# Last expert's rows weighed and scattered straight to the output; attention product, loads, weighing and stores placed between expert steps

## The chip, the cores and the metric

The kernel runs on one core of one Trainium2 chip. The metric is the time of one execution on the device, in microseconds (us).

## The reference

A normalized input goes through two branches that are added to it: linear attention with a learned feature map, and a mixture of eight experts of which each token takes two. S = 2048 tokens, D = 512, 32 heads of 16, F = 1792.

```python
# x: (1, 2048, 512)
xn = layernorm(x)
# attention branch
q, k, v = split_heads(xn @ wqkv)
phi_q = concat(softmax(q @ w_phi), softmax(-(q @ w_phi)))      # the same for k
num = phi_q @ (phi_k^T v);  den = phi_q . sum(phi_k) + 1e-6
A = merge_heads(num / den) @ wo
# expert branch
gates = softmax(xn @ wg); take the top 2 of 8, divided by their sum -> cw
y_e = gelu(xn @ w1[e]) @ w2[e]
B = sum over the two experts of cw * y_e
return x + A + B
```

## The kernel before

All matrix products run in three passes over split operands (a high and a low part, `hi*hi + lo*hi + hi*lo`, `mm3`, lines L162 to L164), so a logical product of 512 columns is three matmuls.

**Stages.** The first part normalizes, computes queries, keys, values and gates, and sorts tokens into slots of experts. Experts are then taken in order of size, each with a fixed number of rows (its cap). One of four plans of caps is chosen at run time by a branch; each has its own copy ("arm") of the code below. In the runs here it is the first: 556, 544, 540, 528, 520, 512, 504, 492.

**Steps.** Each expert has 14 steps (`FB`), one for 128 of the 1792 hidden columns, so there are steps s = 0 to 111. A step issues, in this order: `load_we(s+5)` on SP (weights), `split_we(s+2)` (ACT cast L256, DVE subtraction L259, the high and low parts), `layer1(s)` (12 matmuls into a bank pH, gelu on ACT L1171, cast L1173, DVE subtraction L1176 giving the split h), then a list of other work put there with `at(step, function, ...)`, then `layer2(s-1)`. An expert whose cap is at most 512 uses `layer2_rows`: 12 matmuls of 512 columns (L1211) that add into four banks pY of 128 rows; in the expert's last step they are sorted by bank, so that a bank is complete every three matmuls. The banks are then copied out, in turn by ACT and DVE (`row_copy`, L1192), and each is scattered by POOL to the DRAM tensor `y_rows`, where each token has its two rows (`scatter`, L1184). For the last expert the four scatters follow at once; for others they are spread over later steps (`leave`).

**Work between the steps.** For each of 16 query blocks u the list holds `q_sub`, `q_exp`, `q_den` and `q_turn` (a DVE transpose, L1118) in steps that follow each other; `numer(c, g)` then takes two transposed blocks: eight matmuls into banks pN (L1135), four from each block. The last, `numer(3,1)`, stands in step 99 and needs the blocks 14 and 15. `load_wo`, `split_wo` bring and split the output weights, `load_r` brings the residual rows, `split_o` splits the attention's result for the output product.

**After the steps.** `attended(t)` for 16 tiles of 128 tokens: 12 matmuls into a bank pO. `load_y(t)` brings both rows of each token of the tile from `y_rows` in one DMA of 512 KB (L1290), which waits for the last scatters; `weigh(t)` scales one row by its gate on ACT (L1474), adds the other with its gate on DVE (L1475) and adds both to the residual (L1477); the bank pO is added (L1469, L1492), and SP stores the tile (L1494).

**Order.** SP, PE, ACT and DVE run in the order in which the code is written; POOL's order comes from the framework's scheduler. Tiles in SBUF come from a pool of slots ("keptN" and "keptR" are two kinds of them).

Of the kernel before, what the change touches and what calls it, by code (L numbers as in the profile page):

```python
# [35 lines left out]
def kernel(  # L36
# [34 lines left out]
    xsr = xs.rearrange("(r a) f -> r (a f)", a=4)  # L71
    xe = nc.dram_tensor("x_slots", (2, STRIDE, D), F32, kind="Internal").ap()
# [1086 lines left out]
    def layer1(s):  # L1159
# [14 lines left out]
        if gw > cap > 4 * P and b == 0:  # L1174
            nc.vector.memset(f32(h[:, cap:gw]), 0.0)
# [15 lines left out]
    def row_copy(i, y, ps):  # L1191
        (nc.vector.tensor_copy if i % 2 else nc.scalar.copy)(  # L1192
            y.rearrange("p (a i c) -> p a i c", a=4, c=32),
            ps.rearrange("p (i a c) -> p a i c", a=4, c=32))

    def layer2_rows(s):

        e, b = divmod(s, FB)
        cap, gw = CAPS[e], GW[e]
        n = -(-cap // P)  # L1200
        m = [min(P, cap - i * P) for i in range(n)]
# [14 lines left out]
        for i in range(n):  # L1216
            if i % 2 == 0:
                y = slot([P, 2, D], name="y")
            row_copy(i, y[0:m[i], i % 2], yb[e][i][0:m[i]])
            to = (y[0:m[i], i % 2], sidx[0:m[i], e * TPE + i:e * TPE + i + 1], ys)  # L1220
            if e == E - 1:
                scatter(*to)
            else:
                at(s + 2 + i, leave, *to)
            if i % 2:
                free(y) if e == E - 1 else at(s + 2 + i, free, y)
        free(*yb.pop(e))

    def layer2(s):
# [3 lines left out]
        if cap <= 4 * P:  # L1233
            return layer2_rows(s)
# [107 lines left out]
    at(94, load_wo)  # L1342
    at(98, split_wo, 0)
    at(99, split_wo, 1)
    for i, t in enumerate((106, 108, 110, 111)):
        at(t, split_o, *divmod(i, 2))

    for i in range(NQ // 2):
        at(max(73 + 3 * i, QS[2 * i + 1] + 6), numer, *divmod(i, 2))
    for t in range(0, NT, 2):  # L1350
        at(106 + t // 4, load_r, t)
# [62 lines left out]
    state = [wraw, wsp, gx, tx, xg, gr, step, kvp, ek, kr, vt, qt, km, qs, ot, oh, ol, ht, yb, scat, xr, yg,  # L1414
# [12 lines left out]
    def experts(caps):  # L1427
# [18 lines left out]


        AHEAD = 8
        EARLY = 4

        def attended(t):
            c, j = divmod(t, TPC)
            ps = bank("pO")
            mm3(ps, [(oh[c, b // 2][:, b % 2, j * P:(j + 1) * P], ol[c, b // 2][:, b % 2, j * P:(j + 1) * P],
                      woh[b // 2][:, b % 2, :], wol[b // 2][:, b % 2, :]) for b in range(KD)])
            if j == TPC - 1:
                for g in range(2):
                    free(oh.pop((c, g)), ol.pop((c, g)))
            return ps

        first = attended(0)
        for t in range(AHEAD):
            load_y(t)
        for g in range(2):
            split_o(2, g)
        for t in range(EARLY):
            o = xr[t // 2][:, t % 2, :]
            ps = attended(t) if t else first
            nc.vector.tensor_add(o, o, ps)  # L1469
            free(ps)  # L1470

        def weigh(t):
            y = yg.pop(t)
            nc.scalar.activation(y[:, 0, :], y[:, 0, :], AF.Copy, scale=cw[:, t, 0:1])  # L1474
            nc.vector.scalar_tensor_tensor(y[:, 0, :], y[:, 1, :], cw[:, t, 1:2], y[:, 0, :], op0=ALU.mult, op1=ALU.add)  # L1475
            o = xr[t // 2][:, t % 2, :].rearrange("p (i a c) -> p i a c", a=4, c=32)
            nc.vector.tensor_add(o, o, y[:, 0, :].rearrange("p (a i c) -> p i a c", a=4, c=32))  # L1477
            free(y)

        late = {}  # L1480
        for t in range(NT + 1):
# [62 lines left out]
```

## Time and profile before

| | |
|---|---|
| median of 3 runs | 881.64 us (881.12 to 882.27) |
| the profiled execution | 881.75 us |
| its span | 879.8 us |
| busy: PE, DVE, ACT, POOL | 870.0, 665.5, 439.0, 148.6 us |
| granted TensorE clock, mean | 0.997 of full speed |
| attention product, first to last matmul | 828.5 to 872.6 us |

The span is the time from the first to the last instruction of the profiled execution; the rest of its own time lies around it. "Busy" counts what an engine executed, and idle time of an engine that nobody waits for costs nothing. The chain that ended last is followed back from the last instruction to what released it at each step.

### The profile page before, as it was taken

The numbers are of one execution on the slowest core, as the hardware profiler recorded it, in microseconds if no ns is written. First come the engines' busy times: TensorE is split into PE (matmuls) and PEld (weight loads), VectorE is DVE, ScalarE is ACT, GpSimd is POOL, SyncE is SP. The second block draws the span as 40 slices with busy tenths as digits, with TensorE's granted clock in tenths as the row PEclk, the third lists the DMA queues.
The fourth block names the chain that finished last, engine by engine and source line by source line (L and its number), as shares of the span: only waits on it lengthen the run. The fifth ranks groups of instructions, "written<-read, shape, count | busy, mean of one in ns | idle before, by whom it ended". The sixth has DMA issues, their size and how long they took to land.

```text
span 879.8 us, 15861 instructions
## 1 busy us (share of the span) xinstructions
PE 870.0 (99%) x5879; PEld 769.8 (87%) x5879; DVE 665.5 (76%) x1089; ACT 439.0 (50%) x721; POOL 148.6 (17%) x201
## 2 busy tenths in 40 slices
PE   9999999999999999999999999999999999999996
PEld 7888878899999999999999999987777778788885
DVE  6889898878774568788779877878887888534477
ACT  4454412734734464556654665645565456544341
POOL 5000002100004113411331141114222200000200
PEclk9999999999999999999999999999999999999998
DMA  8320115674218331843463354425632744750196
GB/s 280 106 96 6 46 34 169 166 210 133 84 59 247 115 114 55 237 124 108 138 212 109 108 189 132 145 89 191 177 123 89 226 140 137 234 194 1 40 343 242
DMA packets 119479, 124.34 MB, mean 141 GB/s; under 512 B 9704, under 2 KB 84200, under 8 KB 119392
## 3 DMA queue, kind: packets, MB, share of 16 engines
q1 hardware_dynamic: 113168, 105.72, 37.6%
q0 software_dynamic: 6224, 17.51, 6.2%
q8 instruction: 48, 0.79, 0.4%
q14 instruction: 39, 0.32, 0.1%
HBM read 97.30 MB, written 25.89 MB: 140 GB/s over the span
## 4 chain that ended last, share of the span: by engine, by line
PE 91%; DVE 5%; issue 1%; DMA 1%; ACT 1%; POOL 0%; SPq 0%; ACTq 0%; DVEq 0%; POOLq 0%
PE pY L1211 13%; PE pH L162 12%; PE pH L163 12%; PE pH L164 12%; PE pY L1246 6%; PE pY L1252 6%; PE pY L1247 6%; PE pY L1249 2%; PE pY L1248 2%; PE pY L1254 2%; PE pV L162 2%; PE pV L164 2%; PE pV L163 2%; PE pQ L451 1%; PE pQ L449 1%; PE pQ L450 1%
## 5 line engine op out<-in xcount | busy, mean ns | idle before, releaser
L1171 ACT ACTIVATE gl<-pH 128x278 f32<-128x278 f32 (+7 forms) x182 | 78.5, 440 | 249.3 <-PE pH L164 239.8
L1176 DVE TENSOR_TENSOR h<-gl,h 128x556 fp32r<-128x556 f32 (+7 forms) x112 | 78.7, 703 | 123.6 <-ACT h L1173 98.4
L1211 PE MATMUL pY<-ws,h 128*128 128x512 f32 x340 | 87.9, 395 | 0.9 <-ACT gl L1171 0.9
L1211 PEld LDWEIGHTS pY<-ws,h 128*128 128x128 f32 x340 | 62.6, 186 | 21.3 <-ACT gl L1171 7.1
L163 PE MATMUL pH<-keptR,ws 128*128 128x270 f32 (+3 forms) x248 | 75.2, 303 | 0.0
L162 PE MATMUL pH<-keptR,ws 128*128 128x270 f32 (+3 forms) x248 | 75.2, 303 | 0.0
L164 PE MATMUL pH<-keptR,ws 128*128 128x270 f32 (+3 forms) x240 | 74.0, 308 | 0.0
L1173 ACT CAST h<-gl 128x556 fp32r<-128x556 f32 (+7 forms) x112 | 70.7, 631 | 3.6
L162 PE MATMUL pH<-xgh,ws 128*128 128x272 f32 (+3 forms) x220 | 70.9, 322 | 0.0
L163 PE MATMUL pH<-xgl,ws 128*128 128x272 f32 (+3 forms) x220 | 70.8, 322 | 0.0
L1184 POOL DMA_INDIRECT y_rows<-keptN,pidx x39 | 43.3, 1110 | 154.8 <-ACT gl L1171 143.3
L1246 PE MATMUL pY<-h,ws 128*128 128x416 f32 (+4 forms) x176 | 62.0, 352 | 0.0
L1184 POOL DMA_INDIRECT y_rows<-keptN,sidx x16 | 19.4, 1210 | 249.4 <-ACT gl L1171 92.2
L164 PE MATMUL pH<-xgh,ws 128*128 128x264 f32 (+3 forms) x188 | 59.7, 318 | 0.0
L1247 PE MATMUL pY<-h,ws 128*128 128x412 f32 (+4 forms) x160 | 55.6, 347 | 0.0
L256 ACT CAST keptR<-keptN 128x1024 fp32r<-128x1024 f32 (+3 forms) x68 | 45.9, 712 | 6.8 <-DVE keptN L952 6.8
L163 PEld LDWEIGHTS pH<-keptR,ws 128*128 128x128 f32 x248 | 46.7, 188 | 2.8
L162 PEld LDWEIGHTS pH<-keptR,ws 128*128 128x128 f32 x248 | 46.8, 189 | 1.8
L164 PE MATMUL pH<-xgh,keptR 128*128 128x272 f32 (+3 forms) x148 | 47.7, 322 | 0.0
L1184 POOL DMA_INDIRECT y_rows<-yq,pidx x27 | 29.4, 1089 | 105.7 <-ACT gl L1171 99.9
L164 PEld LDWEIGHTS pH<-keptR,ws 128*128 128x128 f32 x240 | 45.2, 188 | 1.9
L927 POOL DMA_INDIRECT keptN<-xn_rows,tidx x28 | 31.3, 1117 | 88.3 <-PE pV L164 49.3
(339 smaller groups left out, 2426.7 us busy)
## 6 DMA issues: line engine op xcount, KB each, us to landing
keptN<-in_B_w_dram SPq DMA_DIRECT2D x142, 256.0 KB
wr<-in_B_w_dram SPq DMA_DIRECT2D x82, 256.0 KB
keptN<-y_rows SPq DMA_DIRECT2D x16, 512.0 KB
x_slots<-keptN SPq DMA_DIRECT2D x24, 256.0 KB
keptN<-x_slots SPq DMA_DIRECT2D x40, 128.0 KB
keptN<-in_A_x_dram SPq DMA_DIRECT2D x16, 256.0 KB
xn_rows<-keptN SPq DMA_DIRECT2D x16, 256.0 KB
keptN<-in_A_x_dram SPq DMA_DIRECT2D x8, 512.0 KB
```

What stands on the lines that cost most here:

```text
L162: nc.tensor.matmul(ps, lh, rh, start=(i == 0), stop=False)
L163: nc.tensor.matmul(ps, lh, rl, start=False, stop=False)
L164: nc.tensor.matmul(ps, ll, rh, start=False, stop=(i == n - 1))
L256: nc.scalar.copy(dst_h, src)
L1171: step[:] = [nc.scalar.activation(g[:, c:c + m], ps[:, :m], AF.Gelu_apprx_tanh)]
L1173: nc.scalar.copy(h[:, 0:cap], g)
L1176: nc.vector.tensor_sub(h[:, gw:], g, f32(h[:, 0:cap]))
L1184: i = nc.gpsimd.indirect_dma_start(out=to, out_offset=bass.IndirectOffsetOnAxis(ap=rows, axis=0), in_=y, in_offset=None)
L1211: nc.tensor.matmul(yb[e][i][0:m[i]], h[:, o:o + m[i]], v[z], start=(b == 0 and low + z == 0), stop=(b == FB - 1 and low > 0))
L1246: nc.tensor.matmul(ps[i][:, 0:w - P], vh, h[:, P:w], start=st, stop=False, skip_group_check=True)
L1247: nc.tensor.matmul(ps[i][:, 0:m], vl, h[:, P:cap], start=False, stop=False, skip_group_check=True)
L1252: nc.tensor.matmul(ps[i][:, 0:m], v[0][:, i * P:(i + 1) * P], h[:, gw + P:], start=False, stop=sp_, skip_group_check=True)
```

## The change

The attention product, the loads from `y_rows`, the weighing and the stores no longer stand after the steps. They are spread over the last expert's steps: `attended` over 99 to 106, `load_y` over 99 to 105, `weigh` over 101 to 107, `store` over 102 to 108, with counts for each step. What prepares them stands earlier: `load_wo` (93, was 94), `split_wo` (96 and 97, were 98 and 99), `load_r` (96 to 103, were 106 to 109), `split_o` (98, 100, 102, 103), and `numer(3,1)` in step 97, where it was in 99.

The last expert's rows do not go through `y_rows`. Its rows of `y_rows` are set to zero by four scatters (`last_zero`), so the weighing adds nothing for them. Its gates are gathered by slot into `w7` by way of a small DRAM tensor `cw_rows`. In step 110 the output rows already stored are gathered by slot (`last_base`). When a bank pY of the last expert is complete, one DVE operation computes pY times gate plus base (`last_rows`, L1320 in the changed kernel), and one POOL scatter writes the rows to the output; slots without a token point beyond the output and are dropped by the bounds. The expert before the last now has the four immediate scatters. In the plan that runs, the caps 504 and 492 become 512.

```diff
 PLANS = (
-    (556, 544, 540, 528, 520, 512, 504, 492),
...
+    (556, 544, 540, 528, 520, 512, 512, 512),
...
@@ -1196,9 +1197,7 @@
     def layer2_rows(s):
 
         e, b = divmod(s, FB)
-        cap, gw = CAPS[e], GW[e]
-        n = -(-cap // P)
-        m = [min(P, cap - i * P) for i in range(n)]
+        n = 4
         if b == 0:
             yb[e] = [bank("pY") for _ in range(n)]
         h = ht.pop(s)
...
-            o = low * gw + i * P
-            nc.tensor.matmul(yb[e][i][0:m[i]], h[:, o:o + m[i]], v[z],
+            o = (low * n + i) * P
+            nc.tensor.matmul(yb[e][i], h[:, o:o + P], v[z],
...
         free(h, *ws)
         if b < FB - 1:
             return
         for i in range(n):
+            if e == E - 1:
+                last_rows(i, yb[e][i])
+                continue
             if i % 2 == 0:
                 y = slot([P, 2, D], name="y")
-            row_copy(i, y[0:m[i], i % 2], yb[e][i][0:m[i]])
-            to = (y[0:m[i], i % 2], sidx[0:m[i], e * TPE + i:e * TPE + i + 1], ys)
-            if e == E - 1:
+            row_copy(i, y[:, i % 2], yb[e][i])
+            to = (y[:, i % 2], sidx[:, e * TPE + i:e * TPE + i + 1], ys)
+            if e == E - 2:
                 scatter(*to)
             else:
                 at(s + 2 + i, leave, *to)
             if i % 2:
-                free(y) if e == E - 1 else at(s + 2 + i, free, y)
+                free(y) if e == E - 2 else at(s + 2 + i, free, y)
         free(*yb.pop(e))
 
     def layer2(s):
 
         e, b = divmod(s, FB)
         cap, gw = CAPS[e], GW[e]
-        if cap <= 4 * P:
+        if cap == 4 * P:
             return layer2_rows(s)
         if b == 0:
             yb[e] = [bank("pY") for _ in range(5)]
@@ -1277,6 +1279,55 @@
 
     def leave(y, rows, to):
...
+    LC = (E - 1) * TPE
+    rows7 = cp.tile([P, 3, 4], I32, name="rows7")
+    w7 = cp.tile([P, 4], F32, name="w7")
+
+    def last_index():
+
+        nc.vector.tensor_scalar(rows7[:, 0], sidx[:, LC:LC + 4], float(2 * S - 1), None, op0=ALU.min)
+        nc.vector.tensor_scalar(rows7[:, 1], rows7[:, 0], 1, None, op0=ALU.logical_shift_right)
+        nc.vector.tensor_scalar(rows7[:, 2], sidx[:, LC:LC + 4], 1, None, op0=ALU.logical_shift_right)
+        nc.sync.dma_start(cws.rearrange("(t p i) o -> p t (i o)", p=P, i=2), cw)
...
+    def last_zero(i):
+
+        if i == 0:
+            zero.append(slot([P, D], name="zero"))
+            nc.gpsimd.memset(zero[0], 0.0)
+        paced(scatter(zero[0], sidx[:, LC + i:LC + i + 1], ys))
+        paced(nc.gpsimd.indirect_dma_start(
+            out=w7[:, i:i + 1], out_offset=None, in_=cws,
+            in_offset=bass.IndirectOffsetOnAxis(ap=rows7[:, 0, i:i + 1], axis=0)))
+        if i == 3:
+            free(zero.pop())
+
+    base = {}
+
+    def last_base(i):
+
+        if i % 2 == 0:
+            base[i // 2] = slot([P, 2, D], name="base")
+        nc.gpsimd.indirect_dma_start(
+            out=base[i // 2][:, i % 2, :], out_offset=None, in_=out2,
+            in_offset=bass.IndirectOffsetOnAxis(ap=rows7[:, 1, i:i + 1], axis=0))
+
+    def last_rows(i, ps):
+        o = base[i // 2][:, i % 2, :]
+        nc.vector.scalar_tensor_tensor(o, ps, w7[:, i:i + 1], o, op0=ALU.mult, op1=ALU.add)
+        n = nc.gpsimd.indirect_dma_start(
+            out=out2, out_offset=bass.IndirectOffsetOnAxis(ap=rows7[:, 2, i:i + 1], axis=0), in_=o, in_offset=None,
+            bounds_check=S - 1, oob_is_err=False)
+        for k in done:
+            tc.declare_no_dep(n.ins, k.ins, reason="each token has one slot of the last expert at most")
+        done.append(n)
+        if i % 2:
+            free(base.pop(i // 2))
+
...
-    at(94, load_wo)
-    at(98, split_wo, 0)
-    at(99, split_wo, 1)
-    for i, t in enumerate((106, 108, 110, 111)):
-        at(t, split_o, *divmod(i, 2))
-
+    def attended(t):
+        c, j = divmod(t, TPC)
+        ps = bank("pO")
+        mm3(ps, [(oh[c, b // 2][:, b % 2, j * P:(j + 1) * P], ol[c, b // 2][:, b % 2, j * P:(j + 1) * P],
+                  woh[b // 2][:, b % 2, :], wol[b // 2][:, b % 2, :]) for b in range(KD)])
+        o = xr[t // 2][:, t % 2, :]
+        nc.vector.tensor_add(o, o, ps)
+        free(ps)
+        if j == TPC - 1:
+            for g in range(2):
+                free(oh.pop((c, g)), ol.pop((c, g)))
...
+    def store(t):
+        nc.sync.dma_start(out2[t * P:(t + 1) * P, :], xr[t // 2][:, t % 2, :])
+        if t % 2:
+            free(xr.pop(t // 2))
+
+    at(60, last_index)
+    for i in range(4):
+        at(71 + i, last_zero, i)
+    at(93, load_wo)
+    at(96, split_wo, 0)
+    at(97, split_wo, 1)
     for i in range(NQ // 2):
-        at(max(73 + 3 * i, QS[2 * i + 1] + 6), numer, *divmod(i, 2))
-    for t in range(0, NT, 2):
-        at(106 + t // 4, load_r, t)
+        at(max(73 + 3 * i, QS[2 * i + 1] + 4), numer, *divmod(i, 2))
+    for k in range(NT // 2):
+        at(96 + k, load_r, 2 * k)
+    for g in range(2):
+        at(98, split_o, 0, g)
+
...
+    spread(attended, 99, (2, 2, 2, 2, 4, 2, 1, 1))
+    for c, t in ((1, 100), (2, 102), (3, 103)):
+        for g in range(2):
+            at(t, split_o, c, g)
+    spread(load_y, 99, (4, 2, 2, 2, 3, 2, 1))
+    spread(weigh, 101, (2, 2, 4, 3, 2, 2, 1))
+    spread(store, 102, (2, 2, 4, 3, 2, 2, 1))
+    for i in range(4):
+        at(110, last_base, i)
...
-
-        AHEAD = 8
-        EARLY = 4
-
...
-        first = attended(0)
-        for t in range(AHEAD):
-            load_y(t)
-        for g in range(2):
-            split_o(2, g)
-        for t in range(EARLY):
-            o = xr[t // 2][:, t % 2, :]
-            ps = attended(t) if t else first
-            nc.vector.tensor_add(o, o, ps)
-            free(ps)
...
-        late = {}
-        for t in range(NT + 1):
-            if t < NT:
-                if t >= EARLY:
-                    if t in (EARLY, EARLY + 2):
-                        split_o(3, t // 2 - EARLY // 2)
-                    late[t] = attended(t)
-                weigh(t)
-            if t > 0:
-                o = xr[(t - 1) // 2][:, (t - 1) % 2, :]
-                if t - 1 in late:
-                    ps = late.pop(t - 1)
-                    nc.vector.tensor_add(o, o, ps)
-                    free(ps)
-                nc.sync.dma_start(out2[(t - 1) * P:t * P, :], o)
-                if t % 2 == 0:
-                    free(xr[t // 2 - 1])
-            if t + AHEAD < NT:
-                load_y(t + AHEAD)
-
```

Where instructions stand, at three places. In the rows, DVE_49, PE_49, Activation_49 are waits for those engines, DMAHW and DMASW for transfers of the hardware and software queues; the tiles are named as above.

First place: PE at `numer(3,1)`. In before it follows layer1(99), the first rows of the expert with cap 492, and no row of pN waits for an engine:

```order
L164 MATMUL pH_7916<-xgh_7623,ws_7838 128x492
L1135 MATMUL pN_7934<-keptN_76,keptN_71 32x512 [waits DMAHW5_49,DMAHW2_49,DMAHW1_49]
L1135 MATMUL pN_7935<-keptN_76,keptN_71 32x512 [waits DMAHW4_49,DMAHW3_49]
L1135 MATMUL pN_7934<-keptN_76,keptN_71 32x512 [waits DMAHW6_49]
...
L1135 MATMUL pN_7934<-keptN_74,keptN_71 32x512 [waits DMAHW5_49]
...
L1135 MATMUL pN_7934<-keptN_74,keptN_71 32x512 [waits DMAHW6_49]
...
L1211 MATMUL pY_7947<-ws_7801,h_7874 128x512 [waits Activation_49]
```

In the changed kernel it follows layer1(97), and the first matmul on the second block waits for DVE:

```order
L165 MATMUL pH_7860<-keptR_89,ws_7766 128x512
L1136 MATMUL pN_7880<-keptN_69,keptN_71 32x512
L1136 MATMUL pN_7881<-keptN_69,keptN_71 32x512
...
L1136 MATMUL pN_7880<-keptN_75,keptN_71 32x512 [waits DMAHW0_49,DMASW1_49,DVE_49]
L1136 MATMUL pN_7881<-keptN_75,keptN_71 32x512
L1136 MATMUL pN_7880<-keptN_75,keptN_71 32x512 [waits DMAHW1_49]
...
L1210 MATMUL pY_7309<-ws_7725,h_7820 128x512 [waits Activation_49]
```

DVE around the transpose of that block (keptN_75) in the changed kernel:

```order
L260 TENSOR_TENSOR ws_7817<-wr_7663,keptR_91 128x1024 [waits DMAHW2_49,DMAHW3_49,PE_49,Activation_49]
L1177 TENSOR_TENSOR h_7820<-gl_97,h_7820 128x512 [waits PE_49,Activation_49]
L1119 STREAM_TRANSPOSE keptN_75<-keptN_78 128x16x2x32 [waits DVE_49]
L260 TENSOR_TENSOR keptR_92<-keptN_83,keptR_90 128x1024 [waits DMAHW3_49,DMAHW4_49,DMAHW2_49,DMAHW5_49,DMAHW1_49,DMAHW6_49,DMAHW0_49,DMAHW7_49,PE_49,Activation_49]
L260 TENSOR_TENSOR ws_7856<-wr_7722,ws_7855 128x1024 [waits DMAHW4_49,DMAHW5_49,PE_49,Activation_49]
L1177 TENSOR_TENSOR h_7859<-gl_98,h_7859 128x512 [waits Activation_49]
```

Numer has moved ahead by two steps, the transpose has not.

Second place: PE in step 99 of the changed kernel, between layer1(99) and layer2(98). In before only pY would follow the pH row:

```order
L165 MATMUL pH_7963<-xgh_7636,ws_7856 128x512
L163 MATMUL pO_7980<-keptR_90,keptR_94 128x512 [waits PE_49,Activation_49]
L164 MATMUL pO_7980<-keptR_92,keptR_94 128x512
L165 MATMUL pO_7980<-keptR_90,keptR_89 128x512 [waits DVE_49]
...
L165 MATMUL pO_7994<-woh_7876,otl_7931 128x512
L1210 MATMUL pY_8012<-keptR_91,h_7909 128x512
```

Two tiles of the attention product, 24 matmuls, stand between the two products of the step.

Third place: the end of POOL's arm. In before, the last expert's scatters to y_rows and the branch:

```order
L1184 DMA y_rows<-keptN_88,sidx 11776x512 [waits DMAHW5_49,DMASW4_49,Activation_49]
L1184 DMA y_rows<-keptN_88,sidx 11776x512 [waits DMAHW6_49,DMASW5_49,DVE_49]
L1184 DMA y_rows<-keptN_80,sidx 11776x512 [waits DMASW6_49,Activation_49]
L1184 DMA y_rows<-keptN_80,sidx 11776x512 [waits DMASW7_49,DVE_49]
L1509 UNCONDITIONAL_BRANCH
```

In the changed kernel, the last of the four scatters to y_rows of the expert before, then the gathers of the output rows and the scatters to the output:

```order
L1185 DMA y_rows<-keptN_85,sidx 11776x512 [waits DMASW3_49,DVE_49]
L1314 DMA keptN_77<-out_dram,rows_2012 128x512 [waits DMAHW3_49,DMAHW4_49,DMAHW2_49,DMAHW5_49,DMAHW1_49,DMAHW6_49,DMAHW0_49,DMAHW7_49,DMASW4_49,DVE_49]
L1314 DMA keptN_77<-out_dram,rows_2012 128x512 [waits DMASW5_49]
L1314 DMA keptN_69<-out_dram,rows_2012 128x512 [waits DMASW6_49,DVE_49,PE_49]
L1314 DMA keptN_69<-out_dram,rows_2012 128x512 [waits DMASW7_49,PE_49]
L1321 DMA out_dram<-keptN_77,rows_2012 2048x512 [waits DMASW5_49,DMASW6_49,DMASW4_49,DMASW7_49,DMASW0_49,DVE_49]
L1321 DMA out_dram<-keptN_77,rows_2012 2048x512 [waits DMASW1_49,DVE_49]
L1321 DMA out_dram<-keptN_69,rows_2012 2048x512 [waits DMASW2_49,DVE_49]
L1321 DMA out_dram<-keptN_69,rows_2012 2048x512 [waits DMASW3_49,DVE_49]
L1553 UNCONDITIONAL_BRANCH
```

The branch has moved behind the four scatters that each wait for DVE; in before DVE and SP went on after POOL's branch.

## Rows read from the trace of the kernel before

**Rows 1.** The page's first part: busy time of each engine over the span, its share and its instructions.

```profile
PE 870.0 (99%) x5879; PEld 769.8 (87%) x5879; DVE 665.5 (76%) x1089; ACT 439.0 (50%) x721; POOL 148.6 (17%) x201
```

**Rows 2.** Four stretches, from the last two experts' steps to the end: busy time and number of instructions of PE, PEld, DVE, ACT and POOL, then the granted clock of TensorE, the DMA engines' share and GB/s.

```profile
751.00:826.00 75.00, 75.00 (x344) 60.77 (x343) 31.59 (x38) 34.57 (x52) 3.92 (x4) 1.00 0.36 119
826.00:837.00 11.00, 11.00 (x50) 8.86 (x49) 5.35 (x10) 3.26 (x6) 5.31 (x4) 1.00 0.25 93
837.00:873.00 36.00, 36.00 (x156) 28.86 (x154) 31.09 (x48) 13.45 (x20) 0.00 (x0) 1.00 0.86 330
873.00:880.00 7.00, 0.03 (x1) 0.00 (x0) 1.62 (x3) 0.00 (x0) 0.00 (x0) 0.65 0.31 114
```

**Rows 3.** The chain that ended last: groups of the second layer's product pY (start, us, what). The first six lines are three pairs of neighbouring steps at 512 rows; the next two, with four groups left out between, bound five steps at 504 rows; the last two, with nine left out, bound ten steps at 492 rows.

```profile
611.95 2.79 PE pY L1211 x12
...
617.47 2.77 PE pY L1211 x12
...
629.73 2.78 PE pY L1211 x12
...
635.28 2.73 PE pY L1211 x12
...
647.50 2.77 PE pY L1211 x12
...
652.99 2.72 PE pY L1211 x12
...
718.43 2.75 PE pY L1211 x12
...
745.99 2.75 PE pY L1211 x12
...
768.83 2.74 PE pY L1211 x12
...
823.01 5.52 PE pY L1211 x24
```

**Rows 4.** The same chain at the first matmul of the attention product pO, and PE's last matmul of the run in the list by time (start, duration as modelled, engine, line).

```profile
828.53 0.23 PE pO L162
...
872.63 0.40 PE L164 MATMUL pO<-keptR,keptR 128*128 128x512 f32 x1
```

**Rows 5.** DVE by time around the last q_turn (start, us, line, operation, tiles; idle time before it and its releaser would stand in brackets behind it).

```profile
744.42 0.75 DVE L259 TENSOR_TENSOR xgl<-keptN,xgh 128x256 fp32r<-128x256 f32 x2
745.10 1.22 DVE L259 TENSOR_TENSOR ws<-keptN,ws 128x1024 fp32r<-128x1024 f32 x1
746.23 0.68 DVE L1176 TENSOR_TENSOR h<-gl,h 128x504 fp32r<-128x504 f32 x1
746.82 1.24 DVE L1118 STREAM_TRANSPOSE keptN<-keptN 128x1024 f32<-128x1024 f32 x1
```

**Rows 6.** PE by time where layer1(97) has ended and layer2(96) begins, and the numerator product pN of that query tile in the chain.

```profile
745.82 0.39 PE L1211 MATMUL pY<-ws,h 128*128 128x512 f32 x1
...
756.80 1.02 PE pN L1135 x16
```

**Rows 7.** The last expert's rows by time: ACT's copies of banks 0 and 2 and DVE's of bank 3 (bank 1's is left out), the four scatters on POOL, and SP's first load from y_rows.

```profile
826.49 0.59 ACT L1192 COPY keptN<-pY 128x512 f32<-128x512 f32 x1 [1.19 <-PE pY L1211]
827.87 0.59 ACT L1192 COPY keptN<-pY 128x512 f32<-128x512 f32 x1 [0.79 <-PE pY L1211]
...
828.57 0.69 DVE L1192 COPY keptN<-pY 108x512 f32<-108x512 f32 x1 [0.69 <-PE pY L1211]
...
828.87 1.01 POOL L1184 DMA_INDIRECT y_rows<-keptN,sidx  x1 [52.72 <-ACT keptN L1192]
830.18 2.33 POOL L1184 DMA_INDIRECT y_rows<-keptN,sidx  x1 [0.30 <-DVE otl L259]
832.82 0.97 POOL L1184 DMA_INDIRECT y_rows<-keptN,sidx  x1 [0.30 <-issue]
834.10 1.00 POOL L1184 DMA_INDIRECT y_rows<-keptN,sidx  x1 [0.30 <-issue]
...
837.55 0.34 SPq L1290 DMA_DIRECT2D keptN<-y_rows  x1
```

**Rows 8.** POOL by time at other indirect transfers: a scatter, with the copy on ACT that released it, and gathers that follow each other.

```profile
592.18 0.59 ACT L1192 COPY keptN<-pY 128x512 f32<-128x512 f32 x1 [3.95 <-DVE keptN L1080]
...
593.04 0.97 POOL L1184 DMA_INDIRECT y_rows<-keptN,sidx  x1 [10.03 <-ACT keptN L1192]
594.48 0.98 POOL L927 DMA_INDIRECT gr<-xn_rows,tidx  x1 [0.47 <-ACT gl L1171]
595.76 0.96 POOL L927 DMA_INDIRECT gr<-xn_rows,tidx  x1 [0.30 <-issue]
```

**Rows 9.** DVE's groups by line in the last stretch (busy us, mean ns of one, idle before).

```profile
L1475 DVE SCALAR_TENSOR_TENSOR keptN<-keptN,cw 128x512 f32<-128x512 f32 x16 | 11.9, 746 | 2.3 <-ACT keptN L1474 2.3
...
L1492 DVE TENSOR_TENSOR keptN<-keptN,pO 128x512 f32<-128x512 f32 x12 | 8.1, 680 | 0.0
```

**Rows 10.** The branch at the end of the arm as POOL's and SP's sequencers ran it, and the semaphore instructions of the program's end on SP (count, ns min/median/max, first and last start).

```profile
L1509 POOLq COMPARE_BRANCH  x2: 40/43/46, 147.2 to 830.3; - x2
L1509 SPq COMPARE_BRANCH  x2: 38/48/57, 158.4 to 875.2; - x2
...
L1539 SPq EVENT_SEMAPHORE  x14: 17/28/28, 878.2 to 879.8; - x14
```

More of the change, by code (lines that the diff above doesn't have):

```diff
@@ L71 @@
     xsr = xs.rearrange("(r a) f -> r (a f)", a=4)
+    cws = nc.dram_tensor("cw_rows", (2 * S, 1), F32, kind="Internal").ap()
     xe = nc.dram_tensor("x_slots", (2, STRIDE, D), F32, kind="Internal").ap()
@@ L1173, in layer1 @@
         nc.scalar.copy(h[:, 0:cap], g)
-        if gw > cap > 4 * P and b == 0:
+        if gw > cap and b == 0:
             nc.vector.memset(f32(h[:, cap:gw]), 0.0)
@@ L1279, in leave @@
         paced(scatter(y, rows, to))
+    LC = (E - 1) * TPE
[6 more added lines that the diff above has]
+        nc.sync.dma_start(cws.rearrange("(t p i) o -> p t (i o)", p=P, i=2), cw)
+    zero = []
+    def last_zero(i):
[26 more added lines that the diff above has]
+            free(base.pop(i // 2))
+    done = []
     xr, yg = {}, {}
@@ L1341, with weigh, spread @@
         at(s + 3, q_turn, u)
-    at(94, load_wo)
-    at(98, split_wo, 0)
-    at(99, split_wo, 1)
-    for i, t in enumerate((106, 108, 110, 111)):
-        at(t, split_o, *divmod(i, 2))
-    for i in range(NQ // 2):
-        at(max(73 + 3 * i, QS[2 * i + 1] + 6), numer, *divmod(i, 2))
-    for t in range(0, NT, 2):
-        at(106 + t // 4, load_r, t)
+    def attended(t):
[9 more added lines that the diff above has]
+                free(oh.pop((c, g)), ol.pop((c, g)))
+    def weigh(t):
+        y = yg.pop(t)
+        nc.scalar.activation(y[:, 0, :], y[:, 0, :], AF.Copy, scale=cw[:, t, 0:1])
+        nc.vector.scalar_tensor_tensor(y[:, 0, :], y[:, 1, :], cw[:, t, 1:2], y[:, 0, :], op0=ALU.mult, op1=ALU.add)
+        o = xr[t // 2][:, t % 2, :].rearrange("p (i a c) -> p i a c", a=4, c=32)
+        nc.vector.tensor_add(o, o, y[:, 0, :].rearrange("p (a i c) -> p i a c", a=4, c=32))
+        free(y)
+    def store(t):
[8 more added lines that the diff above has]
+    at(97, split_wo, 1)
+    for i in range(NQ // 2):
+        at(max(73 + 3 * i, QS[2 * i + 1] + 4), numer, *divmod(i, 2))
[3 more added lines that the diff above has]
+        at(98, split_o, 0, g)
+    def spread(f, s0, counts):
+        t = 0
+        for k, n in enumerate(counts):
+            for _ in range(n):
+                at(s0 + k, f, t)
+                t += 1
+        assert t == NT
+    spread(attended, 99, (2, 2, 2, 2, 4, 2, 1, 1))
[7 more added lines that the diff above has]
+        at(110, last_base, i)
     for e in range(1, E):
@@ L1412 @@
     kv_take(0)
-    state = [wraw, wsp, gx, tx, xg, gr, step, kvp, ek, kr, vt, qt, km, qs, ot, oh, ol, ht, yb, scat, xr, yg,
+    state = [wraw, wsp, gx, tx, xg, gr, step, kvp, ek, kr, vt, qt, km, qs, ot, oh, ol, ht, yb, scat, xr, yg, zero, base, done,
              wor, woh, wol, fill, expert, spare, home]
```

16 lines of the change are left out of this document (removed), and 6 rows, old and new, of the table PLANS.

## The prediction

> **What bounds the kernel now.** I read the page's first part, then PE's busy time by stretch, then the chain that ended last, then the other engines by time at the places the change touches. PE is busy 870.0 of 879.8 us [rows 1]. By stretch it is busy 75.00 of 75.00 us in the last two experts' steps and 36.00 of 36.00 us in the attention product, each at a granted clock of 1.00 [rows 2]. So PE sets the pace to its last matmul, and what it is given to do, plus any wait put into it, is the time. Behind it stands a tail: the last matmul of pO begins at 872.63 [rows 4] and, as neighbouring ones follow at 0.23, ends at T = 872.86; the span ends at 879.8, which is T + 6.9. The run took 881.75, so 1.95 us lie outside the span.
>
> **The change, part by part.**
>
> *The attention product moves; it doesn't shrink.* Its 192 matmuls took 872.86 - 828.53 = 44.3 us [rows 4], 0.231 each. Inside steps 99 to 106 they are the same 192 on the same engine, and the steps there have no idle PE to take them in (75.00 of 75.00 [rows 2]). Gain 0 on PE. DVE and ACT bring 31.09 and 13.45 us of work with them, into steps where they are busy 31.59 and 34.57 of 75 us [rows 2]. Over steps and product together DVE is then at (31.59 + 31.09) of 75 + 44, some 53%; that hides them on the average, and a local queue is a rival below.
>
> *Wider caps.* Ten steps at 492 rows took 823.01 - 768.83 = 54.18, or 5.418 each; five at 504 took 27.56, or 5.512 each; three at 512 took 5.52, 5.55 and 5.49, mean 5.52 [rows 3]. Fourteen steps each: 14 x (5.52 - 5.418) + 14 x (5.52 - 5.512) = 1.5. By columns alone it is 14 x 12 x 0.2306 x 20/512 = 1.5 for the one and 0.6 for the other, 2.1. I take **1.7**, bounds 1.5 and 2.1.
>
> *numer(3,1) two steps sooner.* Before, it ran at 756.80 for 1.02 us [rows 6], long after the last q_turn, which ran on DVE from 746.82 for 1.24, to 748.06 [rows 5]. Now it stands right behind layer1(97), and that ended at 745.82 in before [rows 6]. Its first half needs q_turn(14), the second q_turn(15): the row with the DVE wait. The first half runs to 745.82 + 0.51 = 746.33, then PE stands until 748.06: **1.8** us with a little for the signal. DVE can't be sooner, since its rows from 744.42 follow each other without a pause [rows 5] and its order up to the transpose is the same. What queues behind PE is layer2(96) and all that follows, so the stall is lost whole. Bounds: 0 if DVE happened to run ahead, 2.3 if the first half waits too.
>
> *The preparations* (three small DVE operations and a DMA at step 60, a memset, four scatters and four gathers on POOL at steps 71 to 74, four base gathers at 110) are on engines that are not awaited. POOL's instructions take about 1 us each [rows 8] and POOL is busy 3.92 of 75 us there [rows 2]. The base gathers have some 11 us, two steps, before the first use. Cost 0; uncovered, four gathers would be 4 x 1.28 = 5 us. load_wo, load_r, load_y and the stores pass to earlier places in SP's queue. load_y in step 99 waits for the scatters of step 98, with the weights of a step five later behind it; that is 0 unless the wait lasts over about two steps, 11 us.
>
> *The tail.* Now the last matmul is a pY of the last expert. Call its end T'. The last layer2 finishes a bank every three matmuls, so banks are ready at T' - 2.08, - 1.39, - 0.69 and 0; in before ACT took bank 0 at 826.49 and DVE bank 3 at 828.57, where PE turned at 828.53 [rows 7, 4], so the first begins at T' - 2.04. The weighing STT takes 0.75 [rows 9]: T' - 1.29. POOL starts 0.27 after what releases it (592.18 + 0.59 to 593.04 [rows 8]): T' - 1.0. Transfers in a row start 1.28 apart (594.48 to 595.76 [rows 8]), slower than banks come, so the fourth starts at T' + 2.84. In before SP's load that waited for the fourth scatter began 837.55 - 834.10 = 3.45 after it [rows 7]: landed at T' + 6.3. The program's end on SP goes from 878.2 to 879.8 [rows 10], 1.6 more: T' + 7.9, against 6.9 before, **+1.0**. Bounds: had the landing not to be waited for, the scatter's own 1.00 and 0.3 to start SP give T' + 5.7, -1.2; had the four scatters taken what they took in before (copy ended at 827.08, load released at 837.55: 10.47 [rows 7]), it would be -1.29 + 10.47 + 1.6 = T' + 10.8, +3.9. I take the middle, since two things made the four of before slow: the first started 1.8 after its copy and one took 2.33, with DVE's splits beside it; after T' DVE has only the STTs. The Trainium skill, "DMA: Bandwidth & Descriptors", section on the anatomy of one DMA on the SWDGE path, gives about 2.0 us plus bytes over 436e3 for such a transfer; an estimate by it is 2.6 us for 256 KB, where this trace has 3.45 from the scatter's start to the released load; by that figure the sum would be 0.85 us lower.
>
> *Sum.* 1.7 + 1.8 + 1.0 = 4.5 on the profiled run's 881.75: 886.25. The median of the runs, 881.64, lies 0.1 below the profiled one, so I say **886.2 us**. The bounds together give 881.64 + 0.3 to + 8.3, that is 881.9 to 889.9.
>
> **The rivals.** What a measurement here can tell from no change is about 0.2%, 1.8 us.
>
> *(a) Other side: the product hides inside the steps.* If PE had idle time between layer1 and layer2, the 44.3 us would partly fill it. It decides from 4.5 + 1.8 = 6.3 us filled: then the time is under 879.9. All of it filled would give about 842. Against it: 75.00 busy of 75.00 [rows 2] (busy is modelled, but 5.52 for 24 matmuls is 0.230 each, just what pO takes). Chance 0.05.
>
> *(b) No stall, short tail.* Each order of the engines' ends is new. In before SP's branch at the arm's end ran at 875.2 and its closing semaphores only at 878.2 [rows 10], 3.0 us; in the changed kernel SP's last transfer lies steps earlier, so that this branch can be over before T'. If those 3.0 us and not a landing set the old tail, and the new landing is short, the tail is -1.2; with the stall at 0 to 1.8 the time is 881.9 to 884.1. The Trainium skill, "Runtime: NRT & Kernel Launch", section on instruction fetch mechanics, has a taken branch outside the fetched window wait for its code; the 3.0 us here would agree with that, though no row tells it from the wait for the last store. Chance 0.13; a little over half of it is within 0.2%.
>
> *(c) A stall in steps 98 to 107.* Attended(0) in step 99 waits for split_o(0), which DVE does in step 98 behind split_wo and the copy of the late pN; I count 1 to 2 us of slack there. Four products in step 103 meet three or four weighs; each tile is 0.69 + 0.75 + 0.69 of DVE, some 2.1 us, against 2.77 of PE. load_y, slots and banks could each be late by a piece of a step. Price 1 to 6 us on the sum: 887 to 892. For it: DVE's queue is hand-ordered and a late y load blocks it. Against: every load is issued two steps before its weighing. Chance 0.17.
>
> *(d) The tail as the four scatters of before:* 886.2 + 2.9 = 889.1. Chance 0.13.
>
> *That the change does not do what it says:* the plan that runs could be another. It only has larger caps at the last two places of the first plan, so what fitted still fits; under 0.01.
>
> **How the numbers follow.** The forecast itself (numer stall, tail near + 1) 0.51; (a) 0.05, (b) 0.13, (c) 0.17, (d) 0.13. The range leaves out (a), the lower half of (b) and the end of (c) beyond 890.8: 883.0 to 890.8. Cases that are slower by over 0.2% (above 883.4): the forecast, (c), (d) and not quite half of (b), 0.87. Within: 0.08. Faster: (a), 0.05.
>
> **What the changed profile would show.** Steps of the last two experts without extra work at 5.52; a PE gap of about 1.8 right after layer1(97), in the middle of a pN group, released by DVE's transpose; no other PE gap between step 98 and the end; pO matmuls at 0.23 in steps 99 to 106; the last pY matmul near 872.86 + 3.5 = 876.4; four STTs of 0.75 and four scatters at 1.28 behind them; the span's end 7.9 after it. I am wrong if q_turn(15) ends before layer1(97), if PE waits for DVE or a load in steps 98 to 107, or if the end comes less than 6 or more than 10 us after the last matmul.

## The result and the profile after

The changed kernel takes 888.27 us (median of 4 runs, 888.1 to 888.58) where before takes 881.78 beside it: slower by a ratio of 1.0075, 95% interval 1.0057 to 1.0092, that is 6.5 us (5.0 to 8.1). The forecast was 886.2 in 883.0 to 890.8: the time lies inside, the direction is the forecast one, and 2 of the 6.5 us were not in the sum. Now and then an execution falls into a slow state (one of e2 took 1727.63 us, one of e12 1217.01); the medians here leave these two out.

First PE over the whole run and in three stretches (us, busy and number of matmuls, granted clock, DMA share, GB/s): the steps that hold the product, the last steps, and the end.

```profile
PE 874.1 (99%) x5879; PEld 771.1 (87%) x5879; DVE 667.7 (75%) x1094; ACT 437.9 (49%) x719; POOL 159.7 (18%) x214
...
757.00:823.00 66.00, 66.00 (x287) 1.00 0.60 212
823.00:869.00 46.00, 46.00 (x200) 1.00 0.42 143
877.00:887.00 10.00, 1.27 (x6) 0.72 0.28 102
```

The number of matmuls is that of [rows 1], and PE is full in the two stretches that hold the steps from 99 on, as it was in [rows 2]: the product was moved, not hidden. PE's list of waits says the same: from 150 us to the end it holds two, neither of them in steps 99 to 111, and one of them is new.

```profile
PE pN L1136 <- DVE keptN L1119: 1.0, 1, 1.0
PE pY L1210 <- ACT gl L1172: 0.9, 1, 0.9
```

The new one, by time on PE and, for DVE's transpose, in the chain:

```profile
747.08 0.40 PE L165 MATMUL pH<-keptR,ws 128*128 128x512 f32 x1
747.41 1.06 PE L1136 MATMUL pN<-keptN,keptN 64*32 64x512 f32 x8
749.47 1.06 PE L1136 MATMUL pN<-keptN,keptN 64*32 64x512 f32 x8 [0.99 <-DVE keptN L1119]
750.46 0.72 PE L1210 MATMUL pY<-ws,h 128*128 128x512 f32 x2
...
748.26 1.17 DVE keptN L1119
```

It is the last numer, right behind layer1(97), released by the transpose that ends at 749.43. From its first row to the next pY it takes 750.46 - 747.41 = 3.05 us, where [rows 6] has 1.02 for the whole of it: 2.03 lost. Each half alone takes 1.06, as long as both did together in before, so the two halves run side by side when nothing parts them. Parted, they take 1.06 each with 0.99 of idle PE between them.

Two starts that lie eight steps apart (three of them with a numer) in the expert that had 504 rows, and three neighbouring starts in the last expert, where the steps hold no other work, in the chain:

```profile
671.58 2.78 PE pY L1210 x12
...
719.69 2.75 PE pY L1210 x12
...
844.90 2.73 PE pY L1210 x12
...
850.43 2.74 PE pY L1210 x12
...
855.94 2.79 PE pY L1210 x12
```

A step at 512 takes 5.53 and 5.51, against 5.418 at 492 [rows 3]. The eight steps take 48.11.

The end: the four weighing operations, the four scatters, PE's last matmul, and SP's closing semaphores.

```profile
876.21 2.85 DVE L1320 SCALAR_TENSOR_TENSOR keptN<-pY,w,keptN 128x512 f32<-128x512 f32 x4 [1.52 <-PE pY L1210]
...
877.87 0.40 PE L1210 MATMUL pY<-keptR,h 128*128 128x512 f32 x1
...
877.24 1.03 POOL L1321 DMA_INDIRECT out_dram<-keptN,rows  x1 [14.47 <-DVE keptN L1320]
878.58 1.00 POOL L1321 DMA_INDIRECT out_dram<-keptN,rows  x1 [0.30 <-DVE keptN L1320]
879.88 0.99 POOL L1321 DMA_INDIRECT out_dram<-keptN,rows  x1 [0.30 <-issue]
881.17 0.98 POOL L1321 DMA_INDIRECT out_dram<-keptN,rows  x1 [0.30 <-issue]
...
L1583 SPq EVENT_SEMAPHORE  x13: 17/28/21697, 862.7 to 886.1; - x13
```

T' is 877.87 + 0.23 = 878.10. The scatters start 1.3 apart, the fourth at T' + 3.1, and the span ends at 886.2, 5.0 after that start and 8.1 after T'. The longest of SP's semaphore instructions lasts 21.7 us from 862.7, so it ends at 884.4, which is 3.2 after the start of the fourth scatter: SP waits for the landing, and 1.8 us of closing instructions follow. In before the span ended 6.9 after T [rows 4], and there SP had no such wait: its longest semaphore instruction took 28 ns [rows 10].

A good part of what is left stands ahead of the experts, where nothing was edited. The matmuls of the value product at 117 to 125 us, by line (busy us, mean ns of one, idle before); first the three lines in before, then the three in the changed kernel:

```profile
L164 PE MATMUL pV<-keptR,xTl 128*128 128x512 f32 x9 | 3.5, 392 | 0.0
L162 PE MATMUL pV<-keptR,xTh 128*128 128x512 f32 x8 | 3.2, 394 | 0.0
L163 PE MATMUL pV<-keptR,xTh 128*128 128x512 f32 x8 | 3.1, 388 | 0.0
```

```profile
L163 PE MATMUL pV<-keptR,xTh 128*128 128x512 f32 x8 | 3.2, 396 | 0.0
L164 PE MATMUL pV<-keptR,xTh 128*128 128x512 f32 x8 | 3.2, 396 | 0.0
L165 PE MATMUL pV<-keptR,xTl 128*128 128x512 f32 x8 | 3.2, 396 | 0.0
```

The code and the order of this stage are those of before, and these matmuls are slower by 0.5 to 2% (388 to 394 against 396 ns). What that costs is seen from the first matmul of pV to the last, in the list by time; before, then the changed kernel:

```profile
30.56 0.40 PE L162 MATMUL pV<-keptR,xTh 128*128 128x512 f32 x1
...
140.77 0.39 PE L164 MATMUL pV<-keptR,xTl 128*128 128x512 f32 x1
```

```profile
30.66 0.40 PE L163 MATMUL pV<-keptR,xTh 128*128 128x512 f32 x1
...
141.46 0.40 PE L165 MATMUL pV<-keptR,xTl 128*128 128x512 f32 x1
```

That is 110.21 against 110.80 us, 0.6 lost.

### The profile page after: what moved, and what is told of

Its sections match the earlier page's. It is cut to its first block, busy times and chain, and to the rows that moved or that the text cites. A ratio compares the mean times of both kernels' runs of the same rounds, so it can differ in the third digit from the quotient of the medians.

```text
span 886.2 us, 15894 instructions
## 1 busy us (share of the span) xinstructions
PE 874.1 (99%) x5879; PEld 771.1 (87%) x5879; DVE 667.7 (75%) x1094; ACT 437.9 (49%) x719; POOL 159.7 (18%) x214
## 4 chain that ended last, share of the span: by engine, by line
PE 91%; DVE 3%; issue 2%; ACT 1%; DMA 1%; POOL 1%; SPq 0%; POOLq 0%; ACTq 0%; DVEq 0%
PE pH L163 12%; PE pH L164 12%; PE pH L165 12%; PE pY L1210 11%; PE pY L1248 6%; PE pY L1249 6%; PE pY L1254 6%; PE pY L1251 2%; PE pY L1250 2%; PE pY L1256 2%; PE pO L163 2%; PE pO L164 2%; PE pO L165 2%; PE pV L163 2%; PE pV L165 2%
## 5 line engine op out<-in xcount | busy, mean ns | idle before, releaser
L1172 ACT ACTIVATE gl<-pH 128x512 f32<-128x512 f32 (+5 forms) x182 | 78.9, 442 | 261.1 <-PE pH L165 260.9
L1177 DVE TENSOR_TENSOR h<-gl,h 128x512 fp32r<-128x512 f32 (+5 forms) x112 | 79.1, 707 | 114.2 <-ACT h L1174 108.9
L1174 ACT CAST h<-gl 128x512 fp32r<-128x512 f32 (+5 forms) x112 | 71.0, 634 | 3.6
L163 PE MATMUL pH<-xgh,ws 128*128 128x272 f32 (+2 forms) x216 | 69.5, 322 | 0.0
L164 PE MATMUL pH<-xgl,ws 128*128 128x272 f32 (+2 forms) x216 | 69.4, 321 | 0.0
L165 PE MATMUL pH<-xgh,ws 128*128 128x264 f32 (+2 forms) x196 | 63.1, 322 | 0.0
L164 PEld LDWEIGHTS pH<-keptR,ws 128*128 128x128 f32 x248 | 46.7, 188 | 2.9
L163 PEld LDWEIGHTS pH<-keptR,ws 128*128 128x128 f32 x248 | 46.7, 188 | 1.8
L1185 POOL DMA_INDIRECT y_rows<-keptN,sidx x12 | 15.2, 1263 | 180.8 <-DMA gr<-xn_rows,tidx 83.1
L165 PE MATMUL pH<-keptR,keptR 128*128 128x260 f32 (+3 forms) x160 | 47.4, 297 | 0.0
L1210 PE MATMUL pY<-keptR,h 128*128 128x512 f32 x172 | 45.4, 396 | 0.0
```

Of the source, the lines that this page charges most:

```text
L163: nc.tensor.matmul(ps, lh, rh, start=(i == 0), stop=False)
L164: nc.tensor.matmul(ps, lh, rl, start=False, stop=False)
L165: nc.tensor.matmul(ps, ll, rh, start=False, stop=(i == n - 1))
L1172: step[:] = [nc.scalar.activation(g[:, c:c + m], ps[:, :m], AF.Gelu_apprx_tanh)]
L1174: nc.scalar.copy(h[:, 0:cap], g)
L1177: nc.vector.tensor_sub(h[:, gw:], g, f32(h[:, 0:cap]))
```

## The experiments

Times are medians, given as the distance to the kernel before as it ran beside them, since before itself differs from group to group: it had 881.62 beside e1 to e4, 882.88 beside e5 to e8, where its runs were more scattered, and 881.87 beside e9 to e12. All four traces of e5 to e8 lose 0.5 to 1.2 us in step 16, which none of their edits touches and where those of the other runs lose at most 0.4; it fits that before was slower there too. The changed kernel is at +6.5. The intervals of two runs that lie 1 to 2 us apart overlap or nearly do, so such a difference is not sharp by the times alone.

**e1: the last numer back in step 99.**

```diff
-        at(max(73 + 3 * i, QS[2 * i + 1] + 4), numer, *divmod(i, 2))
+        at(max(73 + 3 * i, QS[2 * i + 1] + 6), numer, *divmod(i, 2))
```

> The changed kernel with numer(3,1) back in step 99. Theory: the wait for the last transpose is lost whole on PE (in the changed kernel's chain pN takes 3.05 us from its first row to the next pY where other numers take 1.02), so this is 2.0 us faster than the changed kernel, 886.2, with a pN of 1.02 in step 99 and no PE gap. Rival: PE, 2 us earlier, meets the next thing that is late (split_o(0) for the first pO in step 99, a y load), and the time stays at 887.5 to 888.3.

885.99, +4.4 (ratio 1.0049, 1.0037 to 1.0062): 2.1 less than the changed kernel. Its numer, in step 99, is whole again:

```profile
758.59 1.02 PE pN L1136 x16
```

The stall was lost on PE and nothing takes its place.

**e2: caps of 504 and 492 again.** The plans of before; layer 2, the zeroing, the weighing and the scatter use 120 or 108 rows in the last bank.

```diff
-    (556, 544, 540, 528, 520, 512, 512, 512),
+    (556, 544, 540, 528, 520, 512, 504, 492),
...
-        n = 4
+        cap, gw = CAPS[e], GW[e]
+        n = -(-cap // P)
+        m = [min(P, cap - i * P) for i in range(n)]
```

> The changed kernel with the caps 504 and 492 of before (the last rows are then weighed and scattered for 108 rows in the fourth bank). If widening cost what the neighbouring steps at 512 said (the 1.7 of the prediction's sum), 886.6; if the steps of the changed trace are right (1.44 - 0.91 = 0.53 over the expert at 504 and 0.13 a step, 14 steps, over the one at 492, 2.3 together), 886.0; if the wider steps were hidden by other waits, 888.3.

886.55, +4.9 (1.0060, 1.0047 to 1.0073): 1.6 less than the changed kernel by the medians, 1.3 by the ratios. That is nearer to the 1.7 of the sum than to the 2.3 that I read from the changed trace; e7 and e9 show why that reading was too high.

**e3: both undone.** The edits of e1 and e2 together.

> Both of these undone, so that of the change the moved product and the scattered last rows are left. Theory: the two add up, 888.3 - 2.0 - 2.3 = 884.0, which leaves the tail (8.1 us after the last matmul where before had 6.9) and 0.9 us by which the trace of the changed kernel was late ahead of everything the change touches. Rival: they overlap, 885 to 886.

884.88, +3.3 (1.0035, 1.0022 to 1.0048). The caps give 1.1 beside e1, so the two add up to within some 0.5, but 0.9 more than expected stays.

**e4: banks of the last expert in another order,** on top of e3. The last three steps of layer 2 take the banks in another order, the last one with parts that two earlier ones held back; the same matmuls are issued, and the h of the last step takes its slot by another rule.

```diff
+    TURN = {FB - 3: [(FB - 3, 0), (FB - 3, 1)],
+            FB - 2: [(FB - 2, 0), (FB - 2, 1), (FB - 3, 2)],
+            FB - 1: [(FB - 1, 0), (FB - 1, 1), (FB - 2, 2), (FB - 3, 3), (FB - 1, 2), (FB - 2, 3), (FB - 1, 3)]}
...
+        if e == E - 1 and b >= FB - 3:
+            held[b] = h, ws, v
+            for b2, i in TURN.get(b, ()):
+                for low, z in ((0, 0), (0, 1), (1, 0)):
+                    product(b2, i, low, z, held[b2][0], held[b2][2])
```

> As the kernel before this one, and the last expert's last three steps of layer 2 taken bank by bank, so that banks are complete 4.2, 3.5, 1.4 and 0 us before the end of PE instead of 2.1, 1.4, 0.7 and 0; no work more or less. Theory (the tail is the fourth scatter's start plus 3.3 to land plus 1.7): the fourth scatter can start 1.1 after the last matmul instead of 3.1, so 2.0 us less, 882.0. Rival (the tail is set by the code behind the branch, or by the landing of all four): 883.5 to 884.0. If PE has to wait for the last h, up to 1 us of the gain is lost.

883.09, +1.5 (1.0016, 1.0008 to 1.0025): 1.8 less than e3. The first and the last scatter, and PE's last matmul, by time:

```profile
871.45 1.04 POOL L1342 DMA_INDIRECT out_dram<-keptN,rows  x1 [12.09 <-DVE keptN L1341]
...
875.68 1.02 POOL L1342 DMA_INDIRECT out_dram<-keptN,rows  x1 [0.44 <-DVE keptN L1341]
...
874.19 0.39 PE L1217 MATMUL pY<-keptR,h 128*108 128x512 f32 x1
```

The fourth scatter starts 875.68 - 874.42 = 1.3 after the end of PE instead of 3.1, and the span ends at 881.2, 6.8 after the end of PE, where it was 8.9 in e3 and 8.1 in the changed kernel. So the tail hangs on the row of four scatters, and not on something that follows the end of PE by a fixed time. The way from the fourth scatter's start to the end is not fixed either: 5.0 us in the changed kernel, 5.8 in e3, 5.5 here.

**e5: the kernel before with the new plans only** (the four lines of `PLANS` of the change).

> The kernel before, with only the plans of the change (504 and 492 become 512). Undoing the caps gave 1.1 and 1.3 us in the two runs that did it, the steps of the traces say 1.6. If widening has a price of its own whatever stands around it: 882.9 to 883.3. If it was only dear beside the moved product: 881.7.

883.41: the medians differ by 0.5; the ratio is 1.0023 (1.0008 to 1.0038), 0.7 to 3.4 us. Widening has a price of its own, and the times can't say it closer. The trace can, for PE. Two starts in the chain whose fellows in before are 718.43 and 823.01 [rows 3]:

```profile
719.55 2.72 PE pY L1211 x12
...
825.89 5.50 PE pY L1211 x24
```

PE takes 106.34 us between them against 104.58, so widening costs it 1.8. The kernel doesn't lose all of it. PE's last matmul starts at 875.49 and the span ends at 881.6, 5.9 after the end of PE instead of 6.9. DVE's last additions of pO, first before, then e5, by time:

```profile
873.35 1.28 DVE L1492 TENSOR_TENSOR keptN<-keptN,pO 128x512 f32<-128x512 f32 x2
```

```profile
875.92 0.69 DVE L1492 TENSOR_TENSOR keptN<-keptN,pO 128x512 f32<-128x512 f32 x1 [0.80 <-PE pO L164]
```

In before DVE was behind: its last addition ends at 874.63, 1.8 after the end of PE. In e5 it waits for PE and ends 0.9 after it.

**e6: the kernel before with only numer in step 97** (the edit of e1, the other way, on before).

> The kernel before, with only numer(3,1) in step 97. Theory: the wait for the last transpose is lost on PE here too, 2.0 to 2.3 us, so 883.6 to 883.9, with a pN of 3.05 us in the chain. Rival: with the product after the steps something else hides it, 881.6.

884.94, +2.1 (1.0023, 1.0014 to 1.0032). Its chain has the same second half behind the same wait, and the transpose that ends just before it:

```profile
748.16 1.17 DVE keptN L1118
...
749.37 1.06 PE pN L1135 x8
```

e1 and e6 take the edit away and add it alone, and both give 2.1.

**e7: the kernel before with the two small tiles,** which nothing uses.

```diff
+    rows7 = cp.tile([P, 3, 4], I32, name="rows7")
+    w7 = cp.tile([P, 4], F32, name="w7")
+
+    def fill7():
+        nc.vector.memset(rows7, 0)
+        nc.vector.memset(w7, 0.0)
...
+    at(60, fill7)
```

> The kernel before, with only the two small tiles of the change (64 bytes a partition, set to zero in step 60, used by nothing). All five traces of the changed kernel and its variants are 0.6 to 0.8 us late before the first expert, where nothing was edited, and their matmuls at 30 to 42 and 117 to 144 us follow each other at 0.235 where before has 0.226 to 0.229. Theory (the tiles move the buffers behind them in SBUF and that changes these matmuls): 0.3 to 0.8 slower, 882.0 to 882.4, with mean durations of 396 ns on the lines of pV at 117 to 125 us instead of 388 to 394. Rival (the one trace of before was a quick one, or other edits do it): 881.6, with 388 to 394.

884.27, +1.4 (1.0017, 1.0008 to 1.0025), more than the 0.3 to 0.8 expected. The lines of the value product:

```profile
L164 PE MATMUL pV<-keptR,xTl 128*128 128x512 f32 x8 | 3.2, 396 | 0.0
L163 PE MATMUL pV<-keptR,xTh 128*128 128x512 f32 x8 | 3.2, 395 | 0.0
L162 PE MATMUL pV<-keptR,xTh 128*128 128x512 f32 x8 | 3.2, 395 | 0.0
```

They are those of the changed kernel, in a kernel that computes what before computes in before's order. From the first pV to the last it takes 110.7 us; that is 110.2 in each of the seven traces without tiles of their own and 110.7 to 110.8 in each of the seven with them. The eight steps of the expert at 504 rows are slower too; first before, then e7, in the chain:

```profile
670.66 2.77 PE pY L1211 x12
...
718.43 2.75 PE pY L1211 x12
```

```profile
672.08 2.77 PE pY L1211 x12
...
720.01 2.75 PE pY L1211 x12
```

47.77 against 47.93. So the tiles as such cost time, by what they move or shift: the value product lies long before step 60, the first that uses them. In e5 and e6, without tiles, it has 388 to 394 ns as in before. Not every matmul is slower: between 600 and 745 us the pY matmuls that read slots keptR have a mean of 394 to 396 ns in the traces without tiles of their own and of 396 to 398 in those with them, those that read ws have 394 or 395 in all, and the 48 matmuls of pV that read two slots keptR, at 43 to 54 us, stay at a median of 389.

**e8: e4 with a third tile,** so that what lies behind is 1024 bytes further instead of 64.

```diff
+    pad7 = cp.tile([P, 240], F32, name="pad7")
...
+        nc.vector.memset(pad7[:, 0:4], 0.0)
```

> The kernel e4 with a third small tile, so that the buffers behind lie 1024 bytes a partition further than in before instead of 64. If the pace of those matmuls depends on where the buffers lie within some 1024 bytes or less, it returns to that of before and the time is 0.4 to 0.8 less than e4, 882.3 to 882.7; if not, 883.1.

884.48, +1.6 (1.0016, 1.0003 to 1.0029), as e4 with its ratio of 1.0016, and 395 ns on all three lines of pV. That the pace repeats within 1024 bytes is ruled out for pV. Elsewhere 1024 bytes are not the same as 64: the eight steps at 504 rows take 47.66 us here, less than in before, and between steps 17 and 57 the trace loses 0.4 us that e4 does not lose.

**e9: the changed kernel with its tiles inside one that is dead.**

```diff
-    rows7 = cp.tile([P, 3, 4], I32, name="rows7")
-    w7 = cp.tile([P, 4], F32, name="w7")
+    lg = logits.rearrange("p t e -> p (t e)")
+    rows7 = lg[:, 0:12].bitcast(I32).rearrange("p (a b) -> p a b", a=3)
+    w7 = lg[:, 12:16]
```

> The changed kernel with its two small tiles laid into the gate logits' tile, which nothing reads after the routing, so that no buffer moves. Theory (the moved buffers cost 0.6 to 0.9 us): the first expert starts within 0.2 us of where it starts in before, the pV lines at 117 to 125 us have 388 to 394 ns, and the time is 5.4 to 5.9 us over the kernel before on the same chip, where the changed kernel was 6.5 over it. Rival (what adding the tiles did was chance or another thing): 6.5 over.

887.17, +5.3 (1.0063, 1.0049 to 1.0077): 1.2 less than the changed kernel. The value product is back at the pace of before:

```profile
L163 PE MATMUL pV<-keptR,xTh 128*128 128x512 f32 x8 | 3.2, 394 | 0.0
L165 PE MATMUL pV<-keptR,xTl 128*128 128x512 f32 x8 | 3.1, 392 | 0.0
L164 PE MATMUL pV<-keptR,xTh 128*128 128x512 f32 x8 | 3.1, 388 | 0.0
```

and the eight steps, here at 512 rows, take 47.84:

```profile
670.78 2.77 PE pY L1210 x12
...
718.62 2.77 PE pY L1210 x12
```

So of the 0.34 that the changed kernel takes longer for them, the tiles make up 0.16 (e7, which adds them) to 0.27 (e9, which takes them away), and I had booked all of it as widening when I wrote what e2 should give.

**e10: e4 with the tiles laid as in e9.**

> e4 (numer in step 99, caps of before, banks in the new order) with the tiles laid into the logits' tile as in e9. e4 was 1.5 us over before; theory: 0.6 to 0.9 less, so 0.6 to 0.9 over; rival: 1.5 over.

882.08, +0.2 (1.0004, 0.9995 to 1.0013), some 1.2 less than e4, again more than expected. With the last numer, the caps, the tiles and the row of scatters put right, the kernel with the moved product is as fast as before within the interval (-0.4 to +1.1 us), and no gain shows.

**e11: e10 with one q_sub a step later; e12: the same on the kernel before.** The traces of before and of e10 have the same gap where an expert ends in step 70.

```diff
-    QS = [FB * (1 + i // 3) + (9, 14, 18)[i % 3] for i in range(NQ)]
+    QS = [FB * (1 + i // 3) + (9, 14, 18)[i % 3] + (i == 10) for i in range(NQ)]
```

> e10 with q_sub of block 10 in step 71 instead of 70 (what follows it moves with it). All traces, before's too, have a PE gap there: PE waits for a gelu that stands on ACT behind the copy of a bank, which waits for DVE's q_sub to give its slot free. Theory: the gap (1.42 between starts where the next to it is 0.23, so 1.2) closes, 0.3 to 0.6 us under before. Rival: another wait takes its place, 0.6 to 0.9 over as e10.

> The kernel before with only that q_sub moved. Theory: 1.2 us under before; rival: unchanged. Beside e11 it tells whether the moved product and the scattered last rows give anything once their side costs are gone: if they give nothing e11 is 0.6 or more over this one; if the shorter tail counts, within 0.3 of it or under.

e11: 880.87, -1.0 (0.9992, 0.9983 to 1.0001); e12: 880.70, -1.2 (0.9986, 0.9977 to 0.9995). PE at that place in before, and in e12:

```profile
594.26 0.97 PE L1211 MATMUL pY<-ws,h 128*128 128x512 f32 x3 [0.95 <-ACT gl L1171]
```

```profile
592.74 0.84 PE L1211 MATMUL pY<-ws,h 128*128 128x512 f32 x3
```

The wait closes in both, and by about the same. With this line the kernel before and the repaired one can't be told apart, so no version here shows a gain from the moved product.

## Why the prediction held, and where its sum fell short

**Right.** PE was the bound and stayed it; the product costs the same inside the steps as behind them (e10 is at +0.2). Rival (a), the product hidden in idle PE, is excluded by 66.00 of 66.00 busy; rival (c), a stall in steps 98 to 107, did not come, since PE's list has no wait there; rival (d) did not come: the fourth scatter started 3.1 after T', not as late as the four of before. Rival (b) did not come: the stall did, and the tail got longer. Its condition, that the branch at the arm's end and not a landing set the old tail, fits the trace of before, where ACT's branch at 867.3 and DVE's at 873.6 are followed by their next instructions at 869.9 and 876.4, 2.6 and 2.8 us later, much as SP's by 3.0, though the stores are all issued by SP; but the new landing was not short.

**Term by term,** forecast and measured: widening 1.7, measured 1.6 and 1.1 by taking it away and 1.8 on PE in e5 (by the steps, 5.52 and 5.418 in the sum and 5.53, 5.51 and 5.418 in the traces); the last numer 1.8, measured 2.1 twice, 2.03 in the trace; the tail +1.0, by the traces 8.1 against 6.9, +1.2; the preparations 0, measured 1.2 when their tiles were laid elsewhere. That makes 5.6 to 6.3 of 6.5, and what is left is within the interval of the ratio. That the time fell inside the range owes something to luck: the range reached that high for the rivals (c) and (d), which did not come, and not for the cost that did.

**The term that the sum put at nothing** is "*The preparations* ... are on engines that are not awaited ... Cost 0". It asked what the new instructions wait for and who waits for them, and that was right. It did not ask what the new tiles do to the rest of the program: 1.2 of the 2 us by which the sum fell short. Half of that, 0.6, is lost in the value product; the rest was not traced term by term.

**A term of a wrong size:** "The first half runs to 745.82 + 0.51 = 746.33". I halved the 1.02 of [rows 6]. A half takes 1.06 alone, as long as the whole, so the loss is all of the time between layer1(97) and the transpose (749.43 - 747.41 = 2.02). By the rows of before that would have been 748.06 - 745.82 = 2.24, which I had as the upper bound and for another reason.

**A reading that fell on the way:** from the changed trace alone I took 2.3 for the widening. It came from comparing steps of two kernels whose buffers lie differently; the runs that change one thing gave 1.1 to 1.6.

**The tail** was right in its sum and nearly so in its parts: the scatters 1.3 apart instead of 1.28, 3.2 from the fourth scatter's start to its landing and 1.8 to the end instead of 3.45 + 1.6. The 6.9 that it was set against is no constant: it holds some 0.9 of DVE's delay, and the traces of e5 and e12 end some 5.9 after PE. The page's figure of the Trainium skill, "DMA: Bandwidth & Descriptors", section on the anatomy of one DMA on the SWDGE path, would have made the sum 0.85 lower and the miss larger; the estimate by it, 2.6 us, is under all landings of these scatters in the changed kernel (3.2 to 4.7), and the measurement decides.

## What to carry to other kernels

Moving work that an engine does without a pause to another place on the same engine gave nothing here, however much it spread the work of others; look first at whether that engine is idle where the work shall go. When an edit adds even 64 bytes of on-chip memory, lay it into something dead, or time the unchanged kernel with the bytes alone, before reading other terms off the traces. When a product is fed by two transposes, a wait between its halves can cost more than the idle time, since the halves may have run side by side.

## What the runs showed of the hardware that was not expected

Two unused tiles, together 64 bytes a partition, made the kernel before 1.4 us slower (0.7 to 2.2), and took matmuls of 128 x 512 in a stage that nobody edited from between 388 and 394 ns to 395 or 396; without tiles of their own (e5, e6, e9 to e12) it is 388 to 394 again, and 1024 bytes do to this stage what 64 do. Of pY, the matmuls that read slots keptR got slower, by some 2 ns, and those that read ws did not. Which buffer it is that must not move, and why its place matters, stays open: the trace names no addresses, and no run here moved one buffer alone.
